# A long convolution by FFT and a rational-function MLP: the conjugate-sign product moved from GpSimd to VectorE, with a signed filter kept in DRAM

## The chip, the cores and the metric

The kernel runs on one NeuronCore of a Trainium2 chip. The metric is the device time of one execution in microseconds (us); lower is better. Five engines work side by side, each with its own instruction queue that runs in order: TensorE (PE in the profile, with its weight loads as PEld), VectorE (DVE), ScalarE (ACT), GpSimd (POOL) and SyncE (SP), which here only issues DMAs. A difference of 0.2% is about the least that a measurement of this kernel can tell from no change.

## The reference

Two stages follow each other. The first is a circular convolution along the sequence, done in the frequency domain; the second is an MLP whose activation is a quotient of two polynomials.

```python
X = np.fft.rfft(x, axis=1)                     # x: (8, 3008, 256)
F = (filt_r + 1j * filt_i)[None, :, :]
y = np.fft.irfft(X * F, n=3008, axis=1)        # real, same shape as x

h = y.reshape(8 * 3008, 256) @ w_in            # w_in: (256, 2048)
P = a[0] + a[1] * h + a[2] * h**2 + a[3] * h**3
Q = 1.0 + np.abs(b[0]) * np.abs(h) + np.abs(b[1]) * h**2
out = (P / (Q + 1e-06)) @ w_out                # w_out: (2048, 256)
```

All values are 32-bit floats.

## The kernel before, in words

**The MLP sets the beat.** The 24064 tokens are cut into 47 tiles of 512, and the hidden width of 2048 into 16 slices of 128. One pair (tile, slice) is a *unit*; there are 752 of them, and `pipeline` starts one in each turn of its loop. A unit `i` first gets six matmuls on TensorE (`product_in`, L458 to L461) that write a PSUM bank, tile `h`. Both factors are split into a high and a low part, which is why there are three products for each half of the inner dimension. Then ScalarE, VectorE and GpSimd evaluate the quotient in nine steps, spread over the following turns by the table `ORDER`: ScalarE takes `|h|`, squares and a reciprocal root (L466 to L488); GpSimd does `pool_q1` (L498) and `pool_m` (L517); VectorE does, in the order of one turn, `g_hi` (L512) for the unit of two turns ago, `rest` (L520) for the unit of three turns ago, `p` (L503) for the unit of one turn ago and `g_lo` (L526) for the unit of three turns ago. In most turns six more matmuls (`product_out`, L535 to L537) follow five turns after the unit's start and read the tiles `hi` and `lo`.

**The convolution is threaded between the units.** For each of the 8 batches it has three stages, each a product with a small constant matrix: stage 1 (`s`, 16 matmul steps), stage 2 (12 steps `y`, the forward transform, and 12 steps `z`, the inverse), stage 3 (`x`, 16 steps, which leave the tiles `xh` and `xl` for `product_in`). Batch 0 runs ahead of the loop (`first_batch`); batches 1 to 7 run as Python generators, and one turn of the loop takes at most one matmul step of them, between `product_in` and `product_out`. A bare `yield` lets one turn go by. A number called `credit` grows by 0.38 a turn (0.6 for batch 1), and each step of the convolution takes 0.86 from it, so that steps come in bursts and are then thinned out.

**Stage 2, which the change touches.** In `product`, the matmul L346 writes the spectrum into a PSUM bank, tile `y`: real parts in partitions 0 to 63, imaginary parts in 64 to 127. VectorE multiplies `y` by the imaginary filter into the filter's own buffer (L353, `z2`), and by the real filter into that one's (L354, `z`). A complex product needs the halves of `z2` swapped and signed: GpSimd does this in four pieces of 64 partitions by 256 columns (L365), each with its own column of signs `sgn_sb`, into a tile `zw`, and adds `zw` to `z` (L370) one turn later. `inverse` multiplies `z` by the inverse matrix (L379) and evicts the result to `ev`; `EV2 = "AV"` says that ScalarE (L261) and VectorE (L263) take turns at it. The filters are read from DRAM again for each batch (L323), each half of the partitions with a DMA of its own, since both halves hold the same values. Batch 0 does it in another way: its filters are signed on the chip (`double_filter`, L331), and a second matrix does the swap (L381).

**Buffers.** Six PSUM banks are shared by `h`, `s`, `y`, `z` and `x`. `Banks.tile` hands out the one with the smallest entry in `free`; `Banks.done(k, later)` enters the present turn plus `later`. `g_lo` enters 1, `product` enters 0.5. So behind a `y` of turn `i`, whose bank is entered as `i + 0.5` in turn `i`, and a `g_lo` of the same turn, entered as `i + 1`, the `product_in` of turn `i + 2` is given the bank of `y`. `f1` and `f2` (the filters) have three buffers each, `zw` has two.

**What sets the order.** On PE, ACT, DVE and POOL the instructions stand as the Python code records them. On SP a scheduler orders the DMA issues by its own estimate of times.

Of the kernel before, what the change touches and what calls it, by code (L numbers as in the profile page):

```python
# [9 lines left out]
F32 = mybir.dt.float32  # L10
# [4 lines left out]
ALU = mybir.AluOpType  # L15
# [12 lines left out]
C = 256  # L28
# [9 lines left out]
PGAP, XGAP = 1, 1  # L38
CPOS = 3
OG = 2  # L40
WAITS = (0, 1)
ORDER = [('g_hi', 2), ('act3', 1), ('act0', 0), ('act4', 1), ('act2', 0), ('act1', 0), ('rest', 3), ('p', 1), ('g_lo', 3), ('pool_m', 2), ('pool_q1', 1), ('pool_q0', 0)]
EV1, EV2, EVO = "A", "AV", "AV"
XB, FB = 4, 3
MINW = float(np.array(897 << 20, np.int32).view(np.float32))
HD = 13
# [52 lines left out]
def conv_moe(ctx: ExitStack, tc: tile.TileContext, xp, fr, fi, w_in, w_out, ab, mats, a1, e, sgn, outT):  # L99
    nc = tc.nc  # L100
# [3 lines left out]
    dram = ctx.enter_context(tc.tile_pool(name="dram", bufs=3, space=DRAM))  # L104
# [8 lines left out]
    sgn_sb = consts.tile([128, 32], F32, name="sgn_sb")[:, :K2]  # L113
# [138 lines left out]

    scr1 = [dram.tile([K2, 128, C], F32, tag="scr1", name=f"scr1_{b}") for b in range(B)]
    scr2 = [dram.tile([N1, 2, K2, C], F32, tag="scr2", name=f"scr2_{b}") for b in range(B)]

    def rows(scr):
        return scr.rearrange("k (g m) c -> (k g) m c", m=NH)
# [48 lines left out]
    class Stage2:  # L306
# [8 lines left out]
        def load_filter(self, q):  # L315
            if self.b == 0 and q >= FB:
                f = tuple(x[:, q - FB] for x in self.more)
            else:
                f = self.tl("f1", q, bufs=FB), self.tl("f2", q, bufs=FB)
            self.f[q] = f  # L320
            for f_, src in zip(f, (fr, fi)):
                for h in range(1 if self.b == 0 else 2):
                    nc.sync.dma_start(f_[64 * h : 64 * h + 64], src[:, 4 * q : 4 * q + 4, :])  # L323

        def double_filter(self, q):
            for f_ in self.f[q][::-1]:
                nc.scalar.activation(f_[64:], f_[:64], AF.Copy)
            f2 = self.f[q][1]
            for k in range(4):
                sg = sgn_sb[:, 4 * q + k : 4 * q + k + 1]  # L330
                nc.gpsimd.tensor_scalar(  # L331
                    out=f2[:, k], in0=f2[:, k], scalar1=sg, scalar2=1.0, op0=ALU.mult, op1=ALU.mult
                )
# [8 lines left out]
        def product(self, i):  # L342
            b, (q, j) = self.b, divmod(i, 2)
            yield 0.86
            bank, yt = banks.tile(f"y_{b}_{i}")
            nc.tensor.matmul(yt, mats_sb[:, 0, :], self.flat(self.tin[q], j), start=True, stop=True)  # L346
            yield
            self.z[i] = z, z2 = [self.flat(f_, j) for f_ in self.f[q]]

            def signed(k):  # L350
                return slice(k * C, k * C + C), sgn_sb[:, 2 * i + k : 2 * i + k + 1]

            nc.vector.tensor_tensor(out=z2, in0=yt, in1=z2, op=ALU.mult)  # L353
            nc.vector.tensor_tensor(out=z, in0=yt, in1=z, op=ALU.mult)  # L354
            banks.done(bank, 0.5)
            if b == 0:

                return

            zw = conv.tile([128, TT], F32, tag="zw", name=f"zw{b}_{i}")  # L360
            for o, n in ((1, 0), (0, 1)):
                o_, n_ = slice(64 * o, 64 * o + 64), slice(64 * n, 64 * n + 64)
                for k in range(2):
                    cs, sg = signed(k)
                    nc.gpsimd.tensor_scalar(  # L365
                        out=zw[o_, cs], in0=z2[n_, cs], scalar1=sg[n_], scalar2=1.0, op0=ALU.mult, op1=ALU.mult
                    )
                if WAITS[n]:
                    yield
            nc.gpsimd.tensor_tensor(out=z, in0=z, in1=zw, op=ALU.add)  # L370

        def inverse(self, i):
# [18 lines left out]
    def stage2(b):  # L391
        s = Stage2(b)
        for q in range(2):
            s.load_filter(q)
            s.load(q)
        for i in range(13):
            if i < 12:
                yield from s.product(i)
            if i > 0:
                yield from s.inverse(i - 1)  # L400
            if i % 2 == 0 and i // 2 + 2 < 6:
                s.load_filter(i // 2 + 2)
                s.load(i // 2 + 2)
            if i > 0 and i % 2 == 0:
                s.store(i // 2 - 1)
# [133 lines left out]
    banks = None  # L539
# [14 lines left out]
    def conv_items(b):  # L554
        for q in range(8):
            yield from stage1(b, q)
        for _ in range(GAP):
            yield
        yield from stage2(b)
# [186 lines left out]
    with tc.manual_schedule(engines=ENGINES):  # L746
        banks = Banks(8 - T * 2 // TT)
# [71 lines left out]
```

## Time and profile before

| what | value |
|---|---|
| time, median of 3 runs (lowest to highest) | 2530.66 us (2528.91 to 2531.14) |
| span of the profiled execution | 2531.5 us |
| PE busy | 2469.1 us, 98% |
| DVE busy | 2267.1 us, 90% |
| ACT busy | 2204.1 us, 87% |
| POOL busy | 1856.6 us, 73% |
| mean DMA rate | 83 GB/s |

The page gives nothing of the profiled execution beside its span, so the span stands for its time; it is 0.8 us above the median of the timed runs. A row of the page's groups reads: line, engine, operation, output tile <- input tiles, shapes, number; then busy time and mean duration of one in ns; then how long the engine stood idle just before these instructions, and what ended it. In a timeline a row is the start, the duration, and the instruction; consecutive starts tell more than durations where instructions overlap.

### The profile page before, as it was taken

To read this page: it belongs to the slowest core of one execution; us is meant where nothing else is said; L and a number is where in the kernel's file an instruction comes from. 1 tells how busy PE (TensorE), PEld (TensorE's weight loads), DVE (VectorE), ACT (ScalarE), POOL (GpSimd) and SP (SyncE) were. 2 spreads that over 40 slices of the span, in tenths; PEclk is the share of its full clock that TensorE was granted. 3 is DMA by queue.
4 is the path that set the end of the run, shared out by engine and by line. 5 is a ranking of instruction groups with operands and counts; after the bars stand their busy time and mean duration, and the time that the engine had idled before them with its cause. 6 is when DMAs were issued, how large, how long until landed. Compare 5 with 4: busy or idle time off the path is not lost.

```text
span 2531.5 us, 35506 instructions
## 1 busy us (share of the span) xinstructions
PE 2469.1 (98%) x10456; PEld 1918.7 (76%) x10456; DVE 2267.1 (90%) x3573; ACT 2204.1 (87%) x4194; POOL 1856.6 (73%) x1984
## 2 busy tenths in 40 slices
PE   5699999999999999999999999999999999999998
PEld 1377777777777777877777777777777778888887
DVE  5789988999889998899888998899988999999998
ACT  4588889888998889988898889988899889999997
POOL 3468876788668876688668886688767887677776
PEclk8899999999999999999999999999999999999999
DMA  8643331333223322232313232223222210000000
GB/s 257 191 137 104 103 113 46 100 103 100 65 80 92 96 82 65 84 103 85 90 53 108 89 94 71 79 82 107 82 65 84 88 55 24 28 24 22 24 9 19
DMA packets 104364, 208.94 MB, mean 83 GB/s; under 512 B 9696, under 2 KB 59104, under 8 KB 104160
## 3 DMA queue, kind: packets, MB, share of 16 engines
q1 hardware_dynamic: 100944, 199.30, 26.0%
q10 hardware_dynamic: 3216, 7.27, 0.9%
q8 instruction: 85, 1.39, 0.2%
q14 instruction: 119, 0.97, 0.1%
HBM read 131.56 MB, written 74.97 MB: 82 GB/s over the span
## 4 chain that ended last, share of the span: by engine, by line
PE 86%; DVE 4%; POOL 3%; issue 1%; ACT 1%; DMA 0%; DVEq 0%; SPq 0%; POOLq 0%; ACTq 0%
PE o L536 12%; PE h_u L458 12%; PE o L535 12%; PE o L537 12%; PE h_u L459 12%; PE h_u L461 12%; PE x L424 4%; PE s L298 4%; PE z L379 3%; PE y L346 2%; POOL q_u L517 1%; DVE h_u L520 1%; POOL zw L365 1%; DVE hi_u L512 1%; DVE h_u L503 1%
## 5 line engine op out<-in xcount | busy, mean ns | idle before, releaser
L517 POOL TENSOR_TENSOR q_u<-q_u,hi_u 128x512 f32<-128x512 f32 x752 | 974.5, 1296 | 489.6 <-DVE hi_u L512 472.2
L535 PE MATMUL o<-hi_u,wo_sb 128*128 128x512 f32 x1504 | 702.9, 467 | 0.0
L466 ACT ACTIVATE q_u<-h_u 128x512 f32<-128x512 f32 x752 | 450.0, 598 | 210.3 <-PE h_u L461 154.3
L520 DVE SCALAR_TENSOR_TENSOR h_u<-h_u,words_sb,q_u 128x512 f32<-128x512 f32 x752 | 565.5, 752 | 59.3 <-POOL q_u L517 58.1
L512 DVE SCALAR_TENSOR_TENSOR hi_u<-h_u,words_sb,a_u 128x512 fp32r<-128x512 f32 x752 | 559.7, 744 | 60.1 <-ACT a_u L488 56.6
L458 PE MATMUL h_u<-xh,wi_sb 128*128 128x512 f32 x1504 | 595.6, 396 | 5.8 <-DVE xl L436 3.9
L536 PE MATMUL o<-lo_u,wo_sb 128*128 128x512 f32 x1504 | 590.0, 392 | 1.6 <-DVE lo_u L526 1.6
L537 PE MATMUL o<-hi_u,wo_sb 128*128 128x512 f32 x1504 | 587.7, 391 | 0.0
L459 PE MATMUL h_u<-xl,wi_sb 128*128 128x512 f32 x1504 | 587.1, 390 | 0.2
L498 POOL TENSOR_SCALAR q_u<-q_u,words_sb 128x512 f32<-128x512 f32 x752 | 584.3, 777 | 2.8 <-ACT a_u L483 2.8
L503 DVE SCALAR_TENSOR_TENSOR h_u<-w_u,words_sb,h_u 128x512 f32<-128x512 f32 x752 | 561.5, 747 | 3.4 <-ACT w_u L473 3.4
L526 DVE TENSOR_TENSOR lo_u<-h_u,a_u 128x512 fp32r<-128x512 f32 x752 | 514.3, 684 | 0.1
L483 ACT ACTIVATE a_u<-q_u 128x512 f32<-128x512 f32 x752 | 475.2, 632 | 0.9 <-DVE lo_u L526 0.7
L488 ACT ACTIVATE a_u<-a_u 128x512 f32<-128x512 f32 x752 | 470.7, 626 | 0.0
L479 ACT ACTIVATE q_u<-q_u 128x512 f32<-128x512 f32 x752 | 469.1, 624 | 0.0
L461 PE MATMUL h_u<-xh,wi_sb 128*128 128x512 f32 x1504 | 463.9, 390 | 0.0
L473 ACT ACTIVATE w_u<-h_u 128x512 f32<-128x512 f32 x752 | 443.8, 590 | 0.3 <-POOL wi_sb L244 0.3
L535 PEld LDWEIGHTS o<-hi_u,wo_sb 128*128 128x128 f32 x1504 | 282.4, 188 | 112.0 <-issue 63.6
L536 PEld LDWEIGHTS o<-lo_u,wo_sb 128*128 128x128 f32 x1504 | 282.7, 188 | 110.2 <-issue 59.9
L458 PEld LDWEIGHTS h_u<-xh,wi_sb 128*128 128x128 f32 x1504 | 282.8, 188 | 80.1 <-DVE lo_u L526 13.2
L459 PEld LDWEIGHTS h_u<-xl,wi_sb 128*128 128x128 f32 x1504 | 282.8, 188 | 63.3 <-issue 3.4
L537 PEld LDWEIGHTS o<-hi_u,wo_sb 128*128 128x128 f32 x1504 | 282.3, 188 | 61.8
(96 smaller groups left out, 1879.6 us busy)
## 6 DMA issues: line engine op xcount, KB each, us to landing
xin<-xp SPq DMA_DIRECT2D x64, 384.0 KB, 3.9
scr<-s1e SPq DMA_DIRECT2D x64, 384.0 KB, 4.1
xin<-scr SPq DMA_DIRECT2D x48, 512.0 KB, 5.2
scr<-ev SPq DMA_DIRECT2D x96, 256.0 KB, 3.9
tl<-scr SPq DMA_DIRECT2D x64, 384.0 KB, 3.2
outT<-oe SPq DMA_DIRECT2D x47, 512.0 KB, 2.7
f<-fr SPq DMA_DIRECT2D x87, 256.0 KB, 4.1
f<-fi SPq DMA_DIRECT2D x87, 256.0 KB, 3.9
```

The source lines that it names most:

```text
L458: nc.tensor.matmul(o, w_in_part(0, f, cc), xh[:, cc, ts], start=cc == 0, stop=False)
L459: nc.tensor.matmul(o, w_in_part(0, f, cc), xl[:, cc, ts], start=False, stop=False)
L461: nc.tensor.matmul(o, w_in_part(1, f, cc), xh[:, cc, ts], start=False, stop=cc == 1)
L498: nc.gpsimd.tensor_scalar(out=self.q, in0=self.q, scalar1=AIK, scalar2=SGN, op0=ALU.mult, op1=ALU.add)
L503: v.scalar_tensor_tensor(out=H, in0=w, scalar=PK, in1=H, op0=ALU.add, op1=ALU.mult)
L512: nc.vector.scalar_tensor_tensor(out=self.hi, in0=self.H, scalar=self.p0, in1=self.a, op0=ALU.add, op1=ALU.mult)
L517: nc.gpsimd.tensor_tensor(out=self.q, in0=self.q, in1=self.hi.bitcast(F32), op=ALU.mult)
L520: nc.vector.scalar_tensor_tensor(out=self.H, in0=self.H, scalar=self.p0, in1=self.q, op0=ALU.add, op1=ALU.subtract)
L526: nc.vector.tensor_tensor(out=self.lo, in0=self.H, in1=self.a, op=ALU.mult)
L535: nc.tensor.matmul(o, w_out_part(0, f, dd), self.hi, start=f == 0, stop=False)
L536: nc.tensor.matmul(o, w_out_part(0, f, dd), self.lo, start=False, stop=False)
L537: nc.tensor.matmul(o, w_out_part(1, f, dd), self.hi, start=False, stop=f == 15)
```

## The change

- **The sign.** A new function `sign` multiplies the imaginary filter's buffer by the signs, in place, on GpSimd, two pieces of 128 partitions by 256 columns for each product. Only batch 1 does it, one product ahead, and writes each signed block of the filter (`q` = 0 to 5, 512 KB) to a DRAM tile `fsg[q]` with a DMA on SP. From batch 2 on, `load_filter` reads `fsg[q]` with one DMA where there were two of 256 KB.
- **The product.** VectorE writes the swapped half-products straight into `zw`: `y` partitions 0 to 63 times the signed filter go to partitions 64 to 127, then the other half. Then comes the bare `yield`, and the product with the real filter follows one turn later, so that one VectorE instruction of 128 partitions becomes two of 64, and the three stand in two turns. `banks.done` for `y` moves with it into the later turn.
- **GpSimd** keeps only the addition, which now stands directly behind the real product in the code, in the same turn as before.
- **The eviction of `z`** is ScalarE's for all steps (`EV2 = "A"`).
- Stage 2 of batch 1 begins two turns later (two bare `yield`s) and signs its first block there.
- Batch 0 is as it was.

```diff
-WAITS = (0, 1)
-EV1, EV2, EVO = "A", "AV", "AV"
+EV1, EV2, EVO = "A", "A", "AV"
...
+    fsg = [dram.tile([128, 4, C], F32, tag=f"fsg{q}", name=f"fsg{q}", bufs=1) for q in range(6)]
...
             for f_, src in zip(f, (fr, fi)):
+                if self.b > 1 and src is fi:
+                    nc.sync.dma_start(f_, fsg[q])
+                    continue
...
+        def sign(self, i):
+            q, j = divmod(i, 2)
+            for k in range(2 * j, 2 * j + 2):
+                nc.gpsimd.tensor_scalar(
+                    out=self.f[q][1][:, k], in0=self.f[q][1][:, k], scalar1=sgn_sb[:, 4 * q + k : 4 * q + k + 1],
+                    scalar2=1.0, op0=ALU.mult, op1=ALU.mult,
+                )
...
-            nc.vector.tensor_tensor(out=z2, in0=yt, in1=z2, op=ALU.mult)
-            nc.vector.tensor_tensor(out=z, in0=yt, in1=z, op=ALU.mult)
-            banks.done(bank, 0.5)
...
             zw = conv.tile([128, TT], F32, tag="zw", name=f"zw{b}_{i}")
-            for o, n in ((1, 0), (0, 1)):
-                o_, n_ = slice(64 * o, 64 * o + 64), slice(64 * n, 64 * n + 64)
-                for k in range(2):
-                    cs, sg = signed(k)
-                    nc.gpsimd.tensor_scalar(
-                        out=zw[o_, cs], in0=z2[n_, cs], scalar1=sg[n_], scalar2=1.0, op0=ALU.mult, op1=ALU.mult
-                    )
-                if WAITS[n]:
-                    yield
+            for n in range(2):
+                o_, n_ = slice(64 - 64 * n, 128 - 64 * n), slice(64 * n, 64 * n + 64)
+                nc.vector.tensor_tensor(out=zw[o_], in0=yt[n_], in1=f2[n_], op=ALU.mult)
+            if b == 1 and i < 11:
+                self.sign(i + 1)
+            if b == 1 and j:
+                nc.sync.dma_start(fsg[q], self.f[q][1])
+            yield
+            nc.vector.tensor_tensor(out=z, in0=yt, in1=z, op=ALU.mult)
+            banks.done(bank, 0.5)
             nc.gpsimd.tensor_tensor(out=z, in0=z, in1=zw, op=ALU.add)
...
+        if b == 1:
+            yield
+            yield
+            s.sign(0)
```

**How the instructions move, on VectorE.** The place is one product of batch 3 (block 1, second half) with the units around it. In the names, `hi_u`, `h_u`, `lo_u`, `q_u`, `w_u`, `a_u` belong to units, `y_3` is the spectrum, `f_1` the filters' buffers, and the last number tells buffers apart. Before:

```order
L512 SCALAR_TENSOR_TENSOR hi_u_7685<-h_u_7598,words_sb,a_u_7614 128x512
L353 TENSOR_TENSOR f_1_7291<-y_3_7677,f_1_7291 128x512
L354 TENSOR_TENSOR f_1_7290<-y_3_7677,f_1_7290 128x512
L520 SCALAR_TENSOR_TENSOR h_u_7560<-h_u_7560,words_sb,q_u_7579 128x512
L503 SCALAR_TENSOR_TENSOR h_u_7628<-w_u_7648,words_sb,h_u_7628 128x512
L526 TENSOR_TENSOR lo_u_7704<-h_u_7560,a_u_7578 128x512
L512 SCALAR_TENSOR_TENSOR hi_u_7721<-h_u_7628,words_sb,a_u_7646 128x512
L520 SCALAR_TENSOR_TENSOR h_u_7598<-h_u_7598,words_sb,q_u_7615 128x512
```

The same place in the changed kernel, where `g_hi` is L524, `rest` L532, `p` L515 and `g_lo` L538, the half-products are L370 and the real product is L376:

```order
L524 SCALAR_TENSOR_TENSOR hi_u_7688<-h_u_7601,words_sb,a_u_7617 128x512
L370 TENSOR_TENSOR zw_3_7695<-y_3_7680,f_1_7306 64x512 x2
L532 SCALAR_TENSOR_TENSOR h_u_7567<-h_u_7567,words_sb,q_u_7586 128x512
L515 SCALAR_TENSOR_TENSOR h_u_7632<-w_u_7652,words_sb,h_u_7632 128x512
L538 TENSOR_TENSOR lo_u_7703<-h_u_7567,a_u_7585 128x512
L524 SCALAR_TENSOR_TENSOR hi_u_7720<-h_u_7632,words_sb,a_u_7650 128x512
L376 TENSOR_TENSOR f_1_7305<-y_3_7680,f_1_7305 128x512
L532 SCALAR_TENSOR_TENSOR h_u_7601<-h_u_7601,words_sb,q_u_7618 128x512
```

The first turn keeps two instructions of the product, now of half height, and the next turn gains one between `g_hi` and `rest`.

**And on GpSimd**, for the same product. `q_u<-q_u,hi_u` is `pool_m`, `q_u<-q_u,words_sb` is `pool_q1`. Before:

```order
L498 TENSOR_SCALAR q_u_7615<-q_u_7615,words_sb 128x512
L365 TENSOR_SCALAR zw_3_7694<-f_1_7291,sgn_sb 64x256 x4
L517 TENSOR_TENSOR q_u_7615<-q_u_7615,hi_u_7685 128x512
L498 TENSOR_SCALAR q_u_7647<-q_u_7647,words_sb 128x512
L370 TENSOR_TENSOR f_1_7290<-f_1_7290,zw_3_7694 128x512
L517 TENSOR_TENSOR q_u_7647<-q_u_7647,hi_u_7721 128x512
```

In the changed kernel `pool_q1` is L510, `pool_m` L529 and the addition L378:

```order
L510 TENSOR_SCALAR q_u_7618<-q_u_7618,words_sb 128x512
L529 TENSOR_TENSOR q_u_7618<-q_u_7618,hi_u_7688 128x512
L510 TENSOR_SCALAR q_u_7651<-q_u_7651,words_sb 128x512
L378 TENSOR_TENSOR f_1_7305<-f_1_7305,zw_3_7695 128x512
L529 TENSOR_TENSOR q_u_7651<-q_u_7651,hi_u_7720 128x512
```

The four pieces are gone; the addition stands where it stood, but its input `f_1` is now finished by VectorE in the same turn, not in the turn before.

More of the change, by code (lines that the diff above doesn't have):

```diff
@@ L347, in product @@
             yield
[L348 to L353, printed above, removed]
+            self.z[i] = z, f2 = [self.flat(f_, j) for f_ in self.f[q]]
+            if b == 0:
+                nc.vector.tensor_tensor(out=f2, in0=yt, in1=f2, op=ALU.mult)
+                nc.vector.tensor_tensor(out=z, in0=yt, in1=z, op=ALU.mult)
+                banks.done(bank, 0.5)
+                return
+            zw = conv.tile([128, TT], F32, tag="zw", name=f"zw{b}_{i}")
+            for n in range(2):
[6 more added lines that the diff above has]
+            yield
             nc.vector.tensor_tensor(out=z, in0=yt, in1=z, op=ALU.mult)
             banks.done(bank, 0.5)
-            if b == 0:
-                return
-            zw = conv.tile([128, TT], F32, tag="zw", name=f"zw{b}_{i}")
-            for o, n in ((1, 0), (0, 1)):
-                o_, n_ = slice(64 * o, 64 * o + 64), slice(64 * n, 64 * n + 64)
-                for k in range(2):
-                    cs, sg = signed(k)
-                    nc.gpsimd.tensor_scalar(
-                        out=zw[o_, cs], in0=z2[n_, cs], scalar1=sg[n_], scalar2=1.0, op0=ALU.mult, op1=ALU.mult
-                    )
-                if WAITS[n]:
-                    yield
             nc.gpsimd.tensor_tensor(out=z, in0=z, in1=zw, op=ALU.add)
```

## The prediction

> **What bounds the kernel now.** I read the page's first and fourth part, then the busy times by stretch, then the waits of each engine, then the timeline of a crowded stretch of stage 2.
>
> ```profile
> PE 2469.1 (98%) x10456; PEld 1918.7 (76%) x10456; DVE 2267.1 (90%) x3573; ACT 2204.1 (87%) x4194; POOL 1856.6 (73%) x1984
> PE 86%; DVE 4%; POOL 3%; issue 1%; ACT 1%; DMA 0%; DVEq 0%; SPq 0%; POOLq 0%; ACTq 0%
> ```
>
> The chain that ended last is TensorE for 86% of the span. A busy TensorE need not be at its peak, so the stretches come next (columns: stretch, its length, busy time and number of PE, PEld, DVE, ACT, POOL, granted clock, DMA share, GB/s).
>
> ```profile
> 0.00:104.00 104.00, 60.57 (x129) 26.08 (x129) 66.12 (x138) 44.18 (x70) 41.60 (x52) 0.82 0.79 243
> 200.00:2200.00 2000.00, 1997.80 (x8524) 1559.33 (x8523) 1814.44 (x2833) 1768.41 (x3376) 1520.49 (x1649) 1.00 0.27 82
> 2200.00:2500.00 300.00, 300.00 (x1358) 250.08 (x1357) 287.30 (x452) 289.07 (x556) 219.32 (x214) 1.00 0.06 20
> ```
>
> Up to 104 us lies batch 0, which the change leaves alone; from about 2100 us on there is no convolution. In between the clock is full and TensorE never rests. What the change can win there is only what TensorE waits for the other engines, so I looked for all its waits from 200 to 2500 us, and for what VectorE waited for:
>
> ```profile
> PEld h_u L458 <- DVE lo_u L526: 12.8, 26, 1.1
> PEld y L346 <- DVE ev L263: 0.7, 1, 0.7
> ...
> DVE h_u L520 <- POOL q_u L517: 57.2, 120, 1.1
> ```
>
> The weight loads of `product_in` wait 26 times for a PSUM bank that `g_lo` has not yet released. VectorE in its turn waits 120 times for GpSimd's `pool_m`. What this costs TensorE shows in the starts of `product_in`:
>
> ```profile
> 783.10 0.39 PE L458 MATMUL h_u<-xh,wi_sb 128*128 128x512 f32 x1
> 786.71 0.49 PE L458 MATMUL h_u<-xh,wi_sb 128*128 128x512 f32 x1
> 790.45 0.39 PE L458 MATMUL h_u<-xh,wi_sb 128*128 128x512 f32 x1
> 793.17 0.39 PE L458 MATMUL h_u<-xh,wi_sb 128*128 128x512 f32 x1
> 800.54 0.40 PE L458 MATMUL h_u<-xh,wi_sb 128*128 128x512 f32 x1
> 806.00 0.39 PE L458 MATMUL h_u<-xh,wi_sb 128*128 128x512 f32 x1
> 810.15 0.50 PE L458 MATMUL h_u<-xh,wi_sb 128*128 128x512 f32 x1 [0.44 <-DVE lo_u L526]
> ...
> 1201.84 0.39 PE L458 MATMUL h_u<-xh,wi_sb 128*128 128x512 f32 x1
> 1205.39 0.39 PE L458 MATMUL h_u<-xh,wi_sb 128*128 128x512 f32 x1
> 1209.00 0.39 PE L458 MATMUL h_u<-xh,wi_sb 128*128 128x512 f32 x1
> ```
>
> A bare turn takes TensorE 2.72 us (790.45 to 793.17), one with a `z` 3.61 (783.10 to 786.71), one with a `y` 3.61 (1205.39 to 1209.00), one with an `x` 3.55 (1201.84 to 1205.39). Where products come as fast as the code lets them, a product takes three turns, `y`, bare and `z`: 9.94 us by these floors. From 790.45 to 800.54 they took 10.09, 0.15 too many. Counted in the order of the program, 34 of the distances from one `y` to the next are such triples: 34 x 0.15 = 5.1 us. Beside them stand single larger stalls, such as the `x` turn from 806.00 to 810.15, which took 4.15, 0.60 over its floor. The bound from above is the weight loads' waiting, 12.8 + 0.7 = 13.5 us. **So some 8 us, an estimate between 5.1 and 13.5, are all that can be won**, 0.3% of the time, whatever VectorE and GpSimd save beyond.
>
> **The change, part by part.** First the engines' sums, from the groups:
>
> ```profile
> L365 POOL TENSOR_SCALAR zw<-f,sgn_sb 64x256 f32<-64x256 f32 x336 | 157.4, 479 | 107.3 <-DVE f L353 44.7 <-issue 42.8 <-POOL q_u L498 11.7
> L331 POOL TENSOR_SCALAR f<-f,sgn_sb 128x256 f32<-128x256 f32 x12 | 5.5, 474 | 8.4 <-ACT f L327 8.4
> L354 DVE TENSOR_TENSOR f<-y,f 128x512 f32<-128x512 f32 x90 | 61.3, 681 | 0.0
> L263 DVE COPY ev<-z 128x512 f32<-128x512 f32 x42 | 28.7, 683 | 0.1
> L261 ACT ACTIVATE ev<-z 128x512 f32<-128x512 f32 x54 | 32.1, 599 | 17.2 <-PE z L379 6.6 <-PE z L381 6.5 <-issue 2.6
> f<-fi SPq DMA_DIRECT2D x87, 256.0 KB, 3.9
> ```
>
> - *GpSimd* loses 336 pieces, 157 us, and gains 24 signings in batch 1 of 0.474 (L331 is of that shape): 11 us.
> - *VectorE* gains 84 instructions, since two half-products take the place of one product. L365 shows that half the partitions do not halve the time (0.479 for 64, 0.474 for 128), so I take 0.68 each as for L354: +57 us; the 42 evictions give back 29. That leaves 28 us more on an engine at 90%.
> - *ScalarE* gains 42 evictions of 0.6, 25 us, in turns with a `z`, where TensorE gives it 3.61 us.
> - *DMA*: six stores of 512 KB, and one load for two of 256 KB 36 times. They stand in SP's queue ahead of loads for blocks two further on, and a load needs some 4 us where a block lasts two products, some 20 us. Nothing.
> - *Two turns' delay in batch 1*: the loop goes on with bare units, so TensorE has work. Nothing.
>
> Whether any of this reaches TensorE is decided in the triples. VectorE there, before:
>
> ```profile
> 789.85 0.74 DVE L512 SCALAR_TENSOR_TENSOR hi_u<-h_u,words_sb,a_u 128x512 fp32r<-128x512 f32 x1
> 790.51 0.68 DVE L353 TENSOR_TENSOR f<-y,f 128x512 f32<-128x512 f32 x1
> 791.11 0.68 DVE L354 TENSOR_TENSOR f<-y,f 128x512 f32<-128x512 f32 x1
> 791.71 0.75 DVE L520 SCALAR_TENSOR_TENSOR h_u<-h_u,words_sb,q_u 128x512 f32<-128x512 f32 x1
> 792.37 0.74 DVE L503 SCALAR_TENSOR_TENSOR h_u<-w_u,words_sb,h_u 128x512 f32<-128x512 f32 x1
> 793.02 0.69 DVE L526 TENSOR_TENSOR lo_u<-h_u,a_u 128x512 fp32r<-128x512 f32 x1
> 793.62 0.74 DVE L512 SCALAR_TENSOR_TENSOR hi_u<-h_u,words_sb,a_u 128x512 fp32r<-128x512 f32 x1
> 794.75 0.76 DVE L520 SCALAR_TENSOR_TENSOR h_u<-h_u,words_sb,q_u 128x512 f32<-128x512 f32 x1 [0.38 <-POOL q_u L517]
> 798.02 0.76 DVE L520 SCALAR_TENSOR_TENSOR h_u<-h_u,words_sb,q_u 128x512 f32<-128x512 f32 x1 [0.61 <-POOL q_u L517]
> ```
>
> and GpSimd beside it:
>
> ```profile
> 791.36 1.97 POOL L365 TENSOR_SCALAR zw<-f,sgn_sb 64x256 f32<-64x256 f32 x4 [0.57 <-DVE f L353]
> 793.41 1.30 POOL L517 TENSOR_TENSOR q_u<-q_u,hi_u 128x512 f32<-128x512 f32 x1
> 795.43 1.30 POOL L370 TENSOR_TENSOR f<-f,zw 128x512 f32<-128x512 f32 x1
> 796.69 1.30 POOL L517 TENSOR_TENSOR q_u<-q_u,hi_u 128x512 f32<-128x512 f32 x1
> ```
>
> By their starts, VectorE's instructions stand closer than they last: from `hi` 0.66, a product 0.60, `rest` 0.66, `p` 0.65, `lo` 0.60; a bare turn is 2.57. The four signings hold `pool_m` until 793.41 and so `rest` until 794.75; then the addition holds the next `pool_m` until 796.69, and `rest` until 798.02. These two waits, 0.38 + 0.61, make the triple 10.09 long: GpSimd sets it.
>
> *The same triple after the change*, from the first half-product at 0: second 0.60, `rest` 1.20, `p` 1.86, `lo` 2.51, `hi` 3.11, real product 3.77, `rest` 4.37, `p` 5.03, `lo` 5.68, `hi` 6.28, and `rest` could start at 6.94. GpSimd's first `pool_m` now waits for nothing, so the first stall goes. The addition is later than before: the real product ends at 3.77 + 0.68 = 4.45, GpSimd takes it up 0.17 later (791.19 to 791.36), 4.62; `pool_m` follows at 5.88 (1.26 later, as 795.43 to 796.69) and ends at 7.18, so `rest` starts at about 7.22, 0.28 late. With the 2.57 that still follow, the next half-product could start at 9.79, under TensorE's 9.94. Then the stalls end.
>
> *The unknown price.* No VectorE instruction of this trace starts at partition 64, or writes other partitions than it reads. Its cost is bounded by two kinds of rows. Cheap: L353 to L354 above, 0.60 from start to start. Dear: a VectorE instruction that needs the end of the one before,
>
> ```profile
> 51.58 0.68 DVE L231 TENSOR_SCALAR dp<-raw 128x512 int32<-128x512 int32 x1
> 52.30 0.70 DVE L232 SCALAR_TENSOR_TENSOR dp<-raw,dp 128x512 int32<-128x512 int32 x1
> ```
>
> 0.72, which is 0.12 more. Three places per product change the partitions: into the first half-product, into the second, and back to `rest`. Dear, the triple is 9.79 + 0.36 = 10.15, 0.21 over TensorE. I take the dear end: every short distance in the trace lies between instructions on the same partitions, and these do not.
>
> [...]
>
> *The bank of `y`* is entered one turn later. By the rule of `Banks`, `product_in` of turn i+2 no longer gets it (i + 1.5) but the bank that `g_lo` of turn i releases (i + 1). This is a new wait: at 793.17 `product_in` started while that `g_lo` (793.02, 0.69 long) still ran until 793.71. Queued behind it are six matmuls and all that follows. Where VectorE is on time it costs nothing; where it is 0.54 late, up to that.
>
> **The sum.** Triples: the two more `y` turns of delay leave 28 of them in the new order. Dear: 28 x 0.21 = 5.9 us stay or come back of the 8, less what the `x` turns let VectorE catch up (its 2.57 and a short `xl` against 3.55); I put the remainder at 4.5, so 3.5 us are won. Profiled span 2531.5 - 3.5 = 2528; the median of the runs lies 0.8 below that span, so **2527 us**, no change that this kernel's measurement (0.2%, 5.1 us) can tell. Chance 0.50.
>
> **Rivals.**
> - *Cheap half-products, the stalls gone*: nearly all of the 8 won, say 6.5: 2524. For it: 9.79 is under 9.94. Against it: the three changes of partitions. Chance 0.28. It is just on the side of faster.
> - *VectorE becomes the bound*: a triple over 10.3, from 0.15 more per product than the dear end. Then 28 triples lose 0.36 (10 us), the 14 distances of four turns about 0.2 (3 us), and the six of two turns, where VectorE has two bare turns and three products of 0.72, 7.3, against TensorE's 6.33, about 0.5 each after the lead (3 us): 16 - 8 = 8 us slower, 2538. For it: the new wait for `g_lo`, and VectorE at 90% beforehand. It decides once VectorE's triple passes the 10.09 of today. Chance 0.15.
> - *The gain doesn't arrive*: TensorE's waits come from VectorE's own load, and GpSimd's relief changes nothing: 2530.7. The 0.99 us of GpSimd waits in one triple speak against it. Chance 0.07.
>
> Faster by over 0.2% (under 2525.6): most of the first rival and a little of the forecast, 0.29. Slower (over 2535.7): the second rival and a little more, 0.17. Within: 0.54. The range, 2522.5 to 2537, takes in both ends of the unknown price and half of the slower case; the forecast's own is 2524.5 to 2530.5.
>
> **What would show it.** VectorE's waits for `pool_m` fall from 57 us to under 30, nearly all behind the addition. From the first to the second half-product: 0.60 or 0.72. A triple of `product_in`: 9.94 (first rival), 9.95 to 10.1 (forecast), over 10.2 (second). GpSimd near 1710 us busy, VectorE near 2300. TensorE's waits for `lo` remain, but now in the turn two behind a `y`. I am wrong if a wait for a DMA (the filters, stage 3's load in batch 1) appears on TensorE or GpSimd, or if the time leaves the range.

## The result, and the profile after

The changed kernel takes **2546.47 us** (median of 5 runs, 2545.82 to 2549.7) against 2530.66 us before: a ratio of 1.0065, 95% interval 1.0055 to 1.0076. It is slower by some 16 us, and the time lies outside the predicted range of 2522.5 to 2537.

The engines' sums came out as predicted. The page's first line for the changed kernel, and its chain that ended last:

```profile
PE 2472.0 (97%) x10456; PEld 1916.7 (75%) x10456; DVE 2306.2 (91%) x3615; ACT 2228.3 (88%) x4236; POOL 1707.3 (67%) x1672
...
PE 87%; DVE 6%; ACT 2%; DMA 2%; issue 1%; POOL 1%; SPq 0%; ACTq 0%; POOLq 0%; DVEq 0%
```

GpSimd 1707 (predicted 1710), VectorE 2306 (2300), ScalarE 24 more. The stretches, with the columns of the prediction's table, say where the time went:

```profile
0.00:104.00 104.00, 60.72 (x130) 26.44 (x130) 66.53 (x138) 44.83 (x72) 41.57 (x52) 0.84 0.82 246
200.00:2200.00 2000.00, 1986.05 (x8451) 1544.71 (x8450) 1838.06 (x2850) 1777.67 (x3389) 1361.33 (x1325) 1.00 0.26 83
2200.00:2500.00 300.00, 300.00 (x1360) 250.21 (x1359) 287.06 (x451) 288.05 (x554) 217.40 (x213) 1.00 0.06 19
```

Batch 0 and the end are as before, and the clock is full. From 200 to 2200 us TensorE is busy 1986.05 us where it was 1997.80: 12 us more idle in this fixed stretch alone. The waits of TensorE's weight loads and of TensorE there (columns: us in total, times, longest):

```profile
PEld h_u L470 <- DVE lo_u L538: 24.5, 36, 1.4
PE h_u L470 <- DVE lo_u L538: 10.8, 16, 1.0
PE z L387 <- DVE f L376: 2.4, 7, 0.4
```

And the groups of VectorE's `rest` and of the half-products over the whole span, as in the prediction's group rows:

```profile
L532 DVE SCALAR_TENSOR_TENSOR h_u<-h_u,words_sb,q_u 128x512 f32<-128x512 f32 x752 | 567.1, 754 | 10.1 <-POOL q_u L529 0.9
L370 DVE TENSOR_TENSOR zw<-y,f 64x512 f32<-64x512 f32 x168 | 115.6, 688 | 26.4 <-PE y L358 21.9
```

VectorE's waits for `pool_m`, 57.2 us before, are 0.9 us: the signings no longer hold it up. This view leaves out short gaps. By the starts of VectorE's instructions after 200 us, `rest` still comes late in 61 places of the changed kernel, by 0.19 us each, 11.7 us together (before: 118 places, 66 us). All of them lie behind a late real product and GpSimd's addition. `product_in` now waits for `g_lo` 24.5 us where it waited 12.8, and `z` now waits for the real product, which it never did. Half the partitions cost VectorE 0.688 us, as much as a whole product (L376, 0.682).

**One such place.** The rows of TensorE in the changed kernel, from one unit's first matmul to that of three units later:

```profile
604.37 0.39 PE L470 MATMUL h_u<-xh,wi_sb 128*128 128x512 f32 x1
...
605.73 1.02 PE L358 MATMUL y<-xin,mats_sb 128*128 128x512 f32 x2
...
607.99 0.39 PE L470 MATMUL h_u<-xh,wi_sb 128*128 128x512 f32 x1
...
610.36 0.50 PE L470 MATMUL h_u<-xh,wi_sb 128*128 128x512 f32 x1 [0.84 <-DVE lo_u L538]
...
612.37 1.10 PE L387 MATMUL z<-f,mats_sb 128*128 128x512 f32 x2 [0.34 <-DVE f L376]
...
616.06 0.39 PE L470 MATMUL h_u<-xh,wi_sb 128*128 128x512 f32 x1
```

and VectorE beside it:

```profile
606.09 0.74 DVE L524 SCALAR_TENSOR_TENSOR hi_u<-h_u,words_sb,a_u 128x512 fp32r<-128x512 f32 x1
606.86 1.41 DVE L370 TENSOR_TENSOR zw<-y,f 64x512 f32<-64x512 f32 x2
608.30 0.76 DVE L532 SCALAR_TENSOR_TENSOR h_u<-h_u,words_sb,q_u 128x512 f32<-128x512 f32 x1
608.97 0.75 DVE L515 SCALAR_TENSOR_TENSOR h_u<-w_u,words_sb,h_u 128x512 f32<-128x512 f32 x1
609.62 0.69 DVE L538 TENSOR_TENSOR lo_u<-h_u,a_u 128x512 fp32r<-128x512 f32 x1
610.22 0.74 DVE L561 TENSOR_SCALAR oe<-o,words_sb 128x512 f32<-128x512 f32 x1
610.88 0.74 DVE L524 SCALAR_TENSOR_TENSOR hi_u<-h_u,words_sb,a_u 128x512 fp32r<-128x512 f32 x1
611.54 0.68 DVE L376 TENSOR_TENSOR f<-y,f 128x512 f32<-128x512 f32 x1
```

Between 607.99 and 610.36 stand only the six matmuls of `product_in`: there is no `product_out` in that turn. This is a line of `pipeline` that the prediction didn't look at:

```python
if done < n and done <= i - LAG and (done % 16 or done == 0 or i >= freed + OG):
    live.pop(done).product_out()
```

With `OG = 2` the first `product_out` of a new tile is put off by a turn, until the accumulators `o` are evicted, and is made up for in the turn after. Counting a tile's turns as f = 0 to 15, from the third tile on the turn f = 5 has none and f = 6 has two. So once per tile TensorE has a turn of 1.36 us, while VectorE has its usual work in it, and the eviction `oe` (L561) besides. In the changed kernel the third `product_in` may not start before `g_lo` of the `y` turn has ended (609.62 + 0.69 = 610.31; it starts at 610.36); its turn before lasted 2.37 us in place of 1.36. Then `z`, which was given the bank of `y`, waits for the real product. Before, the same three turns look like this:

```profile
552.27 0.39 PE L458 MATMUL h_u<-xh,wi_sb 128*128 128x512 f32 x1
...
555.88 0.39 PE L458 MATMUL h_u<-xh,wi_sb 128*128 128x512 f32 x1
...
557.25 0.39 PE L458 MATMUL h_u<-xh,wi_sb 128*128 128x512 f32 x1
...
562.24 0.39 PE L458 MATMUL h_u<-xh,wi_sb 128*128 128x512 f32 x1
```

Here `g_lo` of the `y` turn ended at 557.89 (by its row, 557.21 + 0.68), and `product_in` started at 557.25 all the same, for it had the bank of `y`, which was free from 555.97 on (555.29 + 0.68). Three turns took 9.97 us before and 11.69 after: 1.72 lost. In the order of the program a `y` stands right ahead of a turn without `product_out` nine times after (eight before): 9 x 1.72 = 15.5 us, nearly the whole loss.

To follow all places, I took from each run's trace the distance from one unit's first `product_in` matmul to the next, and subtracted TensorE's floors (1.36 for each six matmuls of a unit, 0.89 for an `s`, `y` or `z`, 0.83 for an `x`). What is left over, summed from the third tile on, in us; the last column is the mean of the three turns (`y`, short turn, double turn with `z`), 9.94 by the floors:

| kernel | turns f = 3 to 8 | other turns | sum | three turns |
|---|---|---|---|---|
| before | 4.2 | 4.1 | 8.3 | 9.97 |
| after | 18.1 | 6.2 | 24.3 | 11.69 |

16.0 us more, which is the loss in time; 13.9 of them stand in the turns f = 3 to 8, since smaller stalls there have gone while the nine came. Theory A, for the experiments: the bank of `y`, held one turn longer, turns VectorE's lateness behind short turns into stalls. Theory B: VectorE's extra work and its held half-products (0.72 apart, not 0.60) cost it, whatever the bank. Theory C: the shift of the products by two turns.

### The profile page after: what moved, and what is told of

The parts are those of the page before. It is cut to its first block, busy times and chain, and to the rows that moved or that the text cites. A ratio compares the mean times of both kernels' runs of the same rounds, so it can differ in the third digit from the quotient of the medians.

```text
span 2545.7 us, 35102 instructions
## 1 busy us (share of the span) xinstructions
PE 2472.0 (97%) x10456; PEld 1916.7 (75%) x10456; DVE 2306.2 (91%) x3615; ACT 2228.3 (88%) x4236; POOL 1707.3 (67%) x1672
## 4 chain that ended last, share of the span: by engine, by line
PE 87%; DVE 6%; ACT 2%; DMA 2%; issue 1%; POOL 1%; SPq 0%; ACTq 0%; POOLq 0%; DVEq 0%
PE o L548 12%; PE h_u L470 12%; PE o L547 12%; PE o L549 12%; PE h_u L471 12%; PE h_u L473 12%; PE x L436 4%; PE s L298 4%; PE z L387 3%; PE y L358 2%; DVE h_u L532 1%; DVE hi_u L524 1%; DVE h_u L515 1%; DMA scr<-s1e 1%; POOL q_u L529 1%
## 5 line engine op out<-in xcount | busy, mean ns | idle before, releaser
L529 POOL TENSOR_TENSOR q_u<-q_u,hi_u 128x512 f32<-128x512 f32 x752 | 973.2, 1294 | 527.0 <-DVE hi_u L524 515.2
L524 DVE SCALAR_TENSOR_TENSOR hi_u<-h_u,words_sb,a_u 128x512 fp32r<-128x512 f32 x752 | 561.8, 747 | 64.2 <-ACT a_u L500 61.6
L470 PE MATMUL h_u<-xh,wi_sb 128*128 128x512 f32 x1504 | 598.5, 398 | 16.0 <-DVE lo_u L538 10.8
L510 POOL TENSOR_SCALAR q_u<-q_u,words_sb 128x512 f32<-128x512 f32 x752 | 580.7, 772 | 2.8 <-ACT a_u L495 2.8
L532 DVE SCALAR_TENSOR_TENSOR h_u<-h_u,words_sb,q_u 128x512 f32<-128x512 f32 x752 | 567.1, 754 | 10.1 <-POOL q_u L529 0.9
L515 DVE SCALAR_TENSOR_TENSOR h_u<-w_u,words_sb,h_u 128x512 f32<-128x512 f32 x752 | 563.3, 749 | 3.4 <-ACT w_u L485 3.4
L538 DVE TENSOR_TENSOR lo_u<-h_u,a_u 128x512 fp32r<-128x512 f32 x752 | 516.4, 687 | 0.1
```

The costliest lines, as they stand in the source:

```text
L470: nc.tensor.matmul(o, w_in_part(0, f, cc), xh[:, cc, ts], start=cc == 0, stop=False)
L510: nc.gpsimd.tensor_scalar(out=self.q, in0=self.q, scalar1=AIK, scalar2=SGN, op0=ALU.mult, op1=ALU.add)
L515: v.scalar_tensor_tensor(out=H, in0=w, scalar=PK, in1=H, op0=ALU.add, op1=ALU.mult)
L524: nc.vector.scalar_tensor_tensor(out=self.hi, in0=self.H, scalar=self.p0, in1=self.a, op0=ALU.add, op1=ALU.mult)
L529: nc.gpsimd.tensor_tensor(out=self.q, in0=self.q, in1=self.hi.bitcast(F32), op=ALU.mult)
L532: nc.vector.scalar_tensor_tensor(out=self.H, in0=self.H, scalar=self.p0, in1=self.q, op0=ALU.add, op1=ALU.subtract)
```

## The experiments

Each kernel was timed beside the kernel before on the same chip (2529.8 to 2530.5 us there); a ratio is to that, with its 95% interval. Line numbers differ a little between the kernels.

**1. The real product at once.** From the changed kernel:

```diff
             for n in range(2):
                 ...
                 nc.vector.tensor_tensor(out=zw[o_], in0=yt[n_], in1=f2[n_], op=ALU.mult)
+            nc.vector.tensor_tensor(out=z, in0=yt, in1=z, op=ALU.mult)
+            banks.done(bank, 0.5)
...
             yield
-            nc.vector.tensor_tensor(out=z, in0=yt, in1=z, op=ALU.mult)
-            banks.done(bank, 0.5)
             nc.gpsimd.tensor_tensor(out=z, in0=z, in1=zw, op=ALU.add)
```

> The changed kernel with the real product put ahead of the turn's end, right behind the two half-products; only GpSimd's addition stays in the next turn. No instruction is added or taken away, VectorE keeps its 2306 us of work and the two changes of partitions; the bank of y is entered in its own turn again. Theory A (the bank of y that is held one turn longer costs the 16 us: at tile boundaries the turn without product_out is over in 1.36 us, and product_in behind it waits for g_lo): the nine pairs of stalls of 1.01 and 0.72 us go, 15 us are won, 2528 to 2533. Theory B (VectorE's 28 us of extra work and its held half-products cost it): nothing changes, 2544 to 2549. Against A could stand that three products in one turn make lo of that turn 0.7 us late for its own bank: then 2533 to 2540.

Measured: 2530.9 us, ratio to before 1.0003 (0.9994 to 1.0012). 15.6 us are won back by moving one instruction within its queue, and the entry of the bank with it. VectorE's work is the same within 6 us, by the page's first line:

```profile
PE 2470.2 (98%) x10456; PEld 1919.2 (76%) x10456; DVE 2300.7 (91%) x3615; ACT 2225.7 (88%) x4236; POOL 1711.2 (68%) x1672
```

and the weight loads wait less, by the waits from 200 to 2200 us:

```profile
PEld h_u L470 <- DVE lo_u L538: 8.0, 15, 1.2
PEld z L387 <- POOL f L378: 3.5, 6, 0.6
```

Theory B falls as an account of the whole. The three turns take 10.38, since `z` in the double turn still waits, now for GpSimd's addition. The edit takes back three things at once: the late entry of the bank, `z`'s wait for the real product, and the lateness of `rest` (no place is left by its starts). So the 15.6 us belong to the three together. Of what TensorE lost over its floors, 11.9 us go in the turns f = 3 to 8 and 3.6 elsewhere. The kernel is only level with before, although GpSimd's relief is in it: something else eats that.

**2. The bank alone.** From the kernel before, no instruction changed:

```diff
             nc.vector.tensor_tensor(out=z, in0=yt, in1=z, op=ALU.mult)
-            banks.done(bank, 0.5)
             if b == 0:
+                banks.done(bank, 0.5)
                 return
...
                 if WAITS[n]:
                     yield
+            banks.done(bank, 0.5)
```

> The kernel before, in which only the entry of y's bank as free is made one turn later (both products stay where they were, no engine gets another instruction). Theory A: product_in two turns behind a y waits for g_lo as in the changed kernel; at 8 tile boundaries a y stands ahead of the turn without product_out, 1.0 to 1.7 us each, and the smaller distances add some: 2539 to 2546, with stalls of about 1 us on the first product_in matmul. Theory B: no work is added, 2530 to 2532.

Measured: 2535.32 us, 1.0021 (1.0011 to 1.0030). The bank by itself costs 5.2 us, by the stall that theory A names, as a row of TensorE's timeline shows:

```profile
557.23 0.50 PE L458 MATMUL h_u<-xh,wi_sb 128*128 128x512 f32 x1 [0.53 <-DVE lo_u L526]
```

at a place where the turn before began at 555.16: 2.07 us for 1.36, 0.71 lost, and eight such places make 5.7. It is less than expected: behind two plain products `g_lo` isn't as late, and `z` doesn't wait, since the real product is already made. That the bank and the half-products act together is a guess here; experiments 6 and 8 test it.

**3. No delay of batch 1.**

```diff
         if b == 1:
-            yield
-            yield
             s.sign(0)
```

> The changed kernel without the two turns' delay in batch 1, so that every product stands in the turn it had before. Theory C (the new phase puts the products in worse turns): the loss goes, 2529 to 2533. Theory A: in the old phase 8 instead of 9 products stand ahead of a turn without product_out, so about 1.7 us are won of 16: 2542 to 2547. Theory B: 2544 to 2549.

Measured: 2541.26 us, 1.0044 (1.0030 to 1.0058). 5.2 us are won, where theory A counted 1.7 for one place fewer and its range ended at 2542; theory C falls as the main cause. The two `yield`s were not free. Of what TensorE lost over its floors, 3.3 us went in the turns f = 3 to 8 and 2.6 elsewhere; which distances between products make up what the one place does not is left open.

**4. VectorE evicts `z` again**, `EV2 = "AV"` in the changed kernel.

> The changed kernel with z evicted by ScalarE and VectorE in turn, as before: VectorE gets 42 evictions more, some 29 us, near 2335, ScalarE 25 us less. Theory A: evictions stand in turns with a z, which last 3.61 us, so little happens: 2545 to 2551. Theory B (VectorE's load sets the time): the load doubles its growth, 2555 to 2565. If the evictions on ScalarE were what costs the time: 2531 to 2540.

Measured: 2551.3 us, 1.0084 (1.0071 to 1.0098): 4.8 us worse, just over theory A's range and well under theory B's. With the bank held, load on VectorE does matter, but 29 us of it cost a sixth of themselves.

**5. No convolution step begun in the turn f = 4** of the changed kernel, so that no `y` stands ahead of a short turn:

```diff
-            elif credit > 0 and i < n and not active and i >= last + PGAP and not (xgen and i > xi):
+            elif credit > 0 and i < n and f != 4 and not active and i >= last + PGAP and not (xgen and i > xi):
```

> The changed kernel with one more condition: no step of the convolution is begun in the turn f = 4, so that no y stands right ahead of the turn without product_out (nine did). The bank is still held one turn longer everywhere, all work is the same. Theory A (held bank, priced only where the turn behind y is short): the nine pairs go, some 12 of the 16 us, and the shorter stalls behind two products two turns apart stay: 2532 to 2537. Theory B (load and held half-products): nothing changes, 2545 to 2549.

Measured: 2544.1 us, 1.0061 (1.0047 to 1.0075), where theory A expected 2532 to 2537. The time is hardly better, yet no `y` stands ahead of a short turn any more. TensorE's waits from 200 to 2200 us:

```profile
PEld h_u L470 <- DVE lo_u L538: 26.8, 74, 1.4
PE h_u L470 <- DVE lo_u L538: 2.9, 7, 0.6
```

Its own waits for `lo` are 2.9 us, 10.8 in the changed kernel; those of the weight loads are many short ones. A stall of another kind has come, in TensorE's timeline:

```profile
359.11 0.39 PE L470 MATMUL h_u<-xh,wi_sb 128*128 128x512 f32 x1
...
366.22 1.91 PE L436 MATMUL x<-e_sb,tl 128*128 128x141 f32 x6 [5.59 <-DMA tl<-scr]
...
369.84 0.39 PE L470 MATMUL h_u<-xh,wi_sb 128*128 128x512 f32 x1
```

Batch 1 has little time, and the turns left free delay its last `z`: it stands in the turn that begins at 354.7, in the changed kernel at 346.0. The load of `tl` for stage 3 is issued at 363.1 in place of 354.3, and TensorE waits for it. This one turn lasts 10.73 us (359.11 to 369.84) and not 3.55: 7.2 us. What is lost over the floors falls from 18.1 to 5.6 in the turns f = 3 to 8, and rises from 6.2 to 14.5 elsewhere, 7.2 of it this wait. Without it the kernel would stand near 2537, the edge of what theory A said; that is worked out, not measured.

**6. One product in place of two halves**, bank held as in the changed kernel; the swap of the halves is left out.

```diff
-            for n in range(2):
-                o_, n_ = slice(64 - 64 * n, 128 - 64 * n), slice(64 * n, 64 * n + 64)
-                nc.vector.tensor_tensor(out=zw[o_], in0=yt[n_], in1=f2[n_], op=ALU.mult)
+            nc.vector.tensor_tensor(out=zw, in0=yt, in1=f2, op=ALU.mult)
```

> The changed kernel with one product over all 128 partitions in place of the two half-products; the swap of the halves is left out, so part of the result is not computed. The bank of y is still held. VectorE loses 84 instructions of some 0.7 us, near 2248, and all changes of partitions. In each pair g_lo ends about 0.7 + 0.36 us earlier, so the stalls of 1.01 shrink to nearly nothing and z's wait with them. Theory A and B agree here that most of the loss goes, 2530 to 2535; if the bank alone mattered, whatever VectorE's work, it would stay at 2544 to 2547.

Measured: 2531.6 us, 1.0006 (0.9997 to 1.0015). With VectorE earlier the held bank costs far less: the stall needs both the bank's rule and VectorE's lateness.

**7. Relief of GpSimd alone**: the kernel before without the four signings.

```diff
-                for k in range(2):
-                    cs, sg = signed(k)
-                    nc.gpsimd.tensor_scalar(...)
                 if WAITS[n]:
                     yield
-            nc.gpsimd.tensor_tensor(out=z, in0=z, in1=zw, op=ALU.add)
+            nc.gpsimd.tensor_tensor(out=z, in0=z, in1=z2, op=ALU.add)
```

> The kernel before with GpSimd's four signings left out (the swap and the signs aren't computed; the addition adds the first product as it is). VectorE, ScalarE, banks and turns stay. This is the relief of GpSimd by itself, which the prediction put at 4.5 us of 8. If that was right: 2525 to 2527. If the triple that it was read from was an unusual one (the 20 triples take 9.98 on the mean, 0.04 over the floor): 2528 to 2530.

Measured: 2524.7 us, 0.9978 (0.9969 to 0.9987): 5.7 us. (The 4.5 in the expectation is not what the prediction said: that was 6.5 for the stalls gone, and 3.5 after the dear hand-over.) The relief was real. But it does not come from the triples, whose mean goes from 9.98 to 9.97. What TensorE loses over its floors falls from 4.2 to 1.0 us in the turns f = 3 to 8, and from 4.1 to 1.5 elsewhere.

**8. The first cure with one product** (edits 1 and 6 together; the swap is left out).

> The first cure (real product in its own turn) with one product over all 128 partitions in place of the two half-products; the swap of the halves is left out, so part of the result is not computed. Bank, turns, signings and evictions are those of the first cure. It prices the half-products by themselves: VectorE loses 84 instructions and the changes of partitions. If they eat the relief that the kernel without signings showed (5.7 us): 2523 to 2526. If the two turns' delay or the evictions eat it: 2529 to 2532, level with the first cure.

Measured: 2524.4 us, 0.9979 (0.9970 to 0.9988). Level with experiment 7, so the DRAM copy, its DMAs, the delay and the evictions cost nothing measurable together once the bank is released in its turn; the half-products cost 6.5 us even then (2530.9 - 2524.4). Each of these times is known to some 2.3 us by its interval, such a difference to some 3.

**9. ScalarE evicts alone**, `EV2 = "A"` in the kernel before.

> The kernel before with z evicted by ScalarE alone, nothing else: VectorE loses 42 evictions, 29 us, ScalarE gains 25. GpSimd's signings stay and with them VectorE's waits for pool_m, which make the stalls of before. Theory A: 2528 to 2531, since evictions stand in turns of 3.61 us. If VectorE's load were what binds: 2522 to 2526. If ScalarE's were: 2532 to 2538.

Measured: 2528.84 us, 0.9995 (0.9986 to 1.0004): no change that can be told.

**10 and 11. A product more, but no change of partitions**: the changed kernel, and the first cure, with the same full product written twice to `zw`; the swap is left out.

```diff
             for n in range(2):
-                o_, n_ = slice(64 - 64 * n, 128 - 64 * n), slice(64 * n, 64 * n + 64)
-                nc.vector.tensor_tensor(out=zw[o_], in0=yt[n_], in1=f2[n_], op=ALU.mult)
+                nc.vector.tensor_tensor(out=zw, in0=yt, in1=f2, op=ALU.mult)
```

> The changed kernel with the two half-products replaced by the same product over all 128 partitions, made twice; the swap of the halves is left out, so part of the result is not computed. As many VectorE instructions as in the changed kernel, the bank of y held one turn longer, but no change of partitions: 0.36 us less per product. If the held hand-overs make g_lo late: stalls of some 0.65 in place of 1.01, and those between two close products nearly gone, 2537 to 2541. If the instruction more does it and the hand-over hardly counts: 2543 to 2547.

> The same with the bank of y released in its own turn (the first cure). Between one product (2524.4) and two half-products (2530.9): if the hand-overs are what costs, 2525 to 2527.5; if the instruction does, 2528.5 to 2531.

Measured: 2541.96 us, 1.0047 (1.0033 to 1.0062), with the bank held; 2528.15 us, 0.9990 (0.9981 to 0.9999), with the bank released. The edit did less than I had thought, as VectorE's timeline in experiment 10 shows:

```profile
604.70 0.74 DVE L523 SCALAR_TENSOR_TENSOR hi_u<-h_u,words_sb,a_u 128x512 fp32r<-128x512 f32 x1
605.41 1.42 DVE L369 TENSOR_TENSOR zw<-y,f 128x512 f32<-128x512 f32 x2
606.74 0.75 DVE L531 SCALAR_TENSOR_TENSOR h_u<-h_u,words_sb,q_u 128x512 f32<-128x512 f32 x1
607.40 0.74 DVE L514 SCALAR_TENSOR_TENSOR h_u<-w_u,words_sb,h_u 128x512 f32<-128x512 f32 x1
608.06 0.68 DVE L537 TENSOR_TENSOR lo_u<-h_u,a_u 128x512 fp32r<-128x512 f32 x1
```

The second product writes the same tile and starts 0.72 behind the first, as the half-products do. The reasons differ: in the trace's records the second full product waits for VectorE's own semaphore, the second half-product for none. So the edit put a wait of the program where it took a change of partitions away, and `lo` starts 3.36 behind `hi` (604.70 to 608.06), against 3.53 in the changed kernel (606.09 to 609.62): 0.17 less, not 0.36. With the bank held those 0.17 are worth 4.5 us (2546.5 to 2542.0), and the instruction more, with that wait on it, 10.4 (2542.0 to 2531.6); with the bank released, 2.8 and 3.8. So with the bank held the added instruction is the larger part; with the bank released the two lie too close to be ranked. What all three changes of partitions cost together is not separated by these runs.

**12 to 15. Versions that might beat both.** All have the first cure. Twice the turn f = 4 is left free of convolution steps: from the start, and from batch 2 on (`f != 4 or nxt == 1`), because of the wait in experiment 5. Once f = 6 is left free in the same way. The last is the second without the delay of batch 1.

> Both cures in one: the real product in the turn of the half-products, and no convolution step begun in the turn f = 4, so that no z stands in the turn f = 6 either (where it still waited some 0.4 us for GpSimd's addition 9 to 11 times). Theory A: 3 to 4 us below the first cure alone, 2526 to 2528, also below the kernel before. Otherwise level with it, 2529 to 2532.

> Both cures again, but the turn f = 4 is left free of convolution steps only from batch 2 on, so that stage 3 of batch 1 doesn't wait for its data (7.2 us once in the other run). By theory A some 3 of the 5 us of stalls that the first cure leaves go (z in the turn f = 6, y in f = 4): 2526 to 2529. If the wait for the data comes back at another batch, 2533 to 2537.

> The first cure, with no convolution step begun in the turn f = 6 from batch 2 on: the y ahead of the short turn stays (with the bank released in its turn), and the z that waited some 0.4 us for GpSimd's addition there is moved one turn on. If that wait is the larger part of what is left: 2526 to 2529. If g_lo's lateness behind the short turn is what costs: 2529 to 2532.

> The real product in its own turn, the turn f = 4 left free from batch 2 on, and no delay of batch 1 by two turns. The distances of two turns between products fall in other places; by the count of turns 10 products stand in f = 5 in place of 12, 10 in f = 6 in place of 7. If the phase does not matter: 2525 to 2528, level with the version with the delay. If it does: 2529 to 2533.

Measured, in this order: 2536.42 us, 1.0026 (1.0015 to 1.0038), with the wait for `tl` in it (5.49 us in its row); **2526.41 us, 0.9988 (0.9979 to 0.9997)**; 2531.66 us, 1.0003 (0.9994 to 1.0012); 2528.23 us, 0.9991 (0.9982 to 1.0001). Of these four, only the second is faster than the kernel before beyond its interval, by 3 us, under the 0.2% that I called the least to be told, and some 20 us below the changed kernel. In the third, a new wait ate what was won: 4.5 us of `product_out`'s weight loads behind the eviction `oe`. Whether the phase counts in the fourth stays open: it is level with the second within the intervals.

What TensorE lost over its floors, as in the table above, and the times:

| kernel | f = 3 to 8 | other | three turns | time |
|---|---|---|---|---|
| 7, before without signings | 1.0 | 1.5 | 9.97 | 2524.7 |
| 8, bank released, one product | 0.9 | 1.4 | 9.97 | 2524.4 |
| 6, bank held, one product | 8.0 | 1.5 | 10.78 | 2531.6 |
| 1, bank released, two halves | 6.2 | 2.6 | 10.38 | 2530.9 |
| after, bank held, two halves | 18.1 | 6.2 | 11.69 | 2546.5 |
| 5, after, no `y` ahead of a short turn | 5.6 | 14.5 | - | 2544.1 |
| 12 to 15, the second | 2.1 | 2.6 | - | 2526.4 |

The rows of 8, 6, 1 and after are a square. The held bank alone (with the real product one turn later) costs 7.2, the half-products alone 6.5, both together 22.1: 8.4 us belong to neither. The sums over the floors, which are read from the traces and not from the times, say the same: 7.2, 6.5 and 22.0. The path from before to after: relief of GpSimd -5.7, the rest of the change about 0, half-products +6.5, bank +15.6, together +16.4 for a measured 16. Such a path adds up by itself, each step being the difference of two runs, so its sum proves nothing; and the shares go by the order. With the bank held first and the half-products behind it, the steps are 7.2 and 14.9.

## Why the prediction was wrong, and where it was right

- **TensorE is the bound, some 8 us can be won: right in size.** Experiment 7 won 5.7, and 8.3 were lost over the floors. *Wrong in place:* I read 0.15 too many from one triple and multiplied by 34. Of the 20 that can be measured it was the longest; their mean is 9.98, 0.04 over the floor. Half of what could be won stood around the short turns.
- **Engines' sums: right**, within some 6 us of the figures named (VectorE grew by 39 us, where the working had 28 and the sign said near 2300). VectorE's waits for `pool_m` fell to 0.9 us, not just under 30. The addition does make `rest` late, by 0.19 where the prediction had 0.28, but in gaps too short for that view.
- **The dear hand-over: right.** The half-products follow each other at 0.72, and all three places that the prediction named took the dear distance (606.09 to 606.86, the pair, and on to 608.30: 0.77, then 0.72 each); the full product of the next turn starts 0.66 behind `hi`, and `rest` 0.60 behind that (610.88, 611.54, 612.14). Over the 84 pairs of the changed kernel's trace the second half starts 0.70 to 0.72 behind the first, and VectorE's next instruction 0.72 to 0.73 behind that. In experiment 10, without the change of partitions, `rest` follows its product by 0.61. That the change of partitions is what holds these instructions was my estimate; the traces show the distances, not the cause. What the half-products were to cost, 4.5 of the 8 us, was mis-sized: they cost 6.5, all of the relief.
- **"The bank of `y` ... Where VectorE is on time it costs nothing; where it is 0.54 late, up to that": the step that failed.** The wait was named, with its place and its releaser, but priced against turns of 2.72 us and more. I had not asked where TensorE's own turn is shorter than VectorE's: one turn per tile has no `product_out` and lasts 1.36 us, and behind it `g_lo` is late even when nothing has gone wrong: by 0.64 us in the kernel before (557.25 to 557.89), where nobody waited for it, and by 1.0 with the half-products. The second half of the price, `z` in the bank of `y`, waiting for the real product, wasn't seen at all. With its two companions the step measured 15.6 us (experiment 1) on top of the half-products, 7.2 with one product in their place, and 5.2 by itself in the kernel before (experiment 2); the sum of the prediction had nothing for it.
- **The delay of two turns, "nothing": wrong by 5.2 us** with the bank held (experiment 3). It sets which products fall ahead of short turns, and by that count 1.7 us are explained; the rest is open. DMA at nothing and the evictions: right, as far as can be told (8, 9).
- **The second rival** had the right sign and both ingredients, but another mechanism: it asked for a VectorE triple over 10.09 everywhere. One dense triple of VectorE after takes 10.06, from `hi` to `hi`, and 0.17 of it is a `rest` that comes 0.83 and not 0.66 behind `hi`, behind the addition:

```profile
295.48 0.75 DVE L524 SCALAR_TENSOR_TENSOR hi_u<-h_u,words_sb,a_u 128x512 fp32r<-128x512 f32 x1
...
298.65 0.75 DVE L524 SCALAR_TENSOR_TENSOR hi_u<-h_u,words_sb,a_u 128x512 fp32r<-128x512 f32 x1
299.48 0.76 DVE L532 SCALAR_TENSOR_TENSOR h_u<-h_u,words_sb,q_u 128x512 f32<-128x512 f32 x1
...
302.18 1.41 DVE L370 TENSOR_TENSOR zw<-y,f 64x512 f32<-64x512 f32 x2
...
305.54 0.74 DVE L524 SCALAR_TENSOR_TENSOR hi_u<-h_u,words_sb,a_u 128x512 fp32r<-128x512 f32 x1
```

- **What would show it**: "waits for `lo` remain, but now in the turn two behind a `y`" came out: by the starts of the weight loads from the third tile on, 27 of 34 late ones stand there, before 0 of 23. What the prediction lacked was the price of a wait at a short turn. Its other sign, the triple of `product_in`, says less: the 18 that lie in full turns take 10.15 on the mean, between the forecast's 10.1 and the second rival's 10.2, but eight of them are at 9.97 or less and four over 10.6.

## What to carry to other kernels

When an edit keeps a shared buffer longer, price it at the shortest turn of the engine that needs it next, not at the usual one: list the turns with less work first (tile boundaries, pauses of an accumulator). A mean or a total of waits says little on what a change adds, and one sampled stretch may be the worst: take the mean over all of its kind. Work added to an engine and a buffer released later can cost more together than one by one (here 22.1 us against 7.2 and 6.5), so release what others need before doing the work that nobody waits for.

## What the hardware showed

- A VectorE instruction of 64 partitions takes 0.688 us, one of 128 takes 0.682 (the rows of L370 above; L376 in the changed kernel's groups): splitting a product by partitions doubled its cost.
- A short wait of TensorE cost a little more than itself: behind the 0.84 us wait above, the first matmul took 0.50 in place of 0.39, and the next one started 0.34 behind it (610.36 to 610.70) in place of 0.23. The long one of experiment 5 cost more: 5.59 us of waiting, and a turn that is 7.2 us too long. The stretches around it (columns as before):

```profile
355.00:360.00 5.00, 5.00 (x20) 3.41 (x19) 4.28 (x8) 3.50 (x8) 4.23 (x5) 1.00 0.31 79
360.00:366.00 6.00, 0.63 (x3) 0.19 (x1) 0.47 (x1) 1.69 (x4) 2.02 (x2) 0.97 0.61 202
366.00:369.00 3.00, 2.78 (x9) 2.62 (x10) 0.26 (x2) 0.84 (x3) 0.00 (x0) 0.50 0.22 76
369.00:372.00 3.00, 3.00 (x17) 2.59 (x16) 2.93 (x5) 2.28 (x5) 0.00 (x0) 0.99 0.00 0
```

After 5.6 us of idling the granted clock is 0.50 in the 3 us from 366 on, and 0.99 in the next 3. The stalls of about 1 us show no such fall: the clock stays at 1.00 over 200 to 2200 us of the changed kernel.
